# Conv + two MLPs on one core: the taps' softmax laid on all channels, warm-up products put first, x turned in transpose mode, block 0's taps shared between VectorE and TensorE

## The chip, the cores and the metric

The kernel runs on 1 core of a Trainium2 chip. The metric is the device time in microseconds, lower is better. PE is TensorE (PEld its weight loads), DVE is VectorE, ACT is ScalarE, POOL is GpSimd, SP is the engine that issues most DMAs (SPq and ACTq are the queues of SP and ACT).

## The reference

```python
# x (2, 4096, 192) f32; weight (8 heads, 7 taps); head h owns channels 24h to 24h+23
w = softmax(weight, axis=-1)                   # exp(w - max) / (sum + 1e-9)
out[s, c] = sum_k w[head(c), k] * x_pad[s + k, c]   # causal, 6 zeros in front
x = out.reshape(8192, 192)
h = x @ w_in;  x = maximum(0.01 * h, h) @ w_out       # 192 -> 2048 -> 192
h = x @ w_in2; g = where(h >= 1, h, where(h <= -1, 0, (h + 1)**2 / 4))
return g @ w_out2
```

## The kernel before, in words

The tokens are cut into 16 blocks of 512 (`T`). In a block the channels lie on the partitions: part 0 holds channels 0 to 127, part 1 the other 64, twice. A block's convolution (`add_conv`) loads x, turns it so that channels lie on partitions (tile `xT`), and adds up seven taps (`tap`: ACT does tap 0, DVE the others, one dependent instruction each at L505). `add_split` then writes the sum as a high half (ACT, L409) and a low half (DVE or POOL, L413) in a reduced format (fp32r), for three to five cheap products instead of one dear one.

A unit `(m, j, f)` is one slice of 128 hidden values of MLP m for block j. It has five "up" products (L549), an activation (ACT twice at L573 and DVE at L577 for the first MLP; the tiles are `gh` and `gl`), and five "down" products (L558). There are 512 units, so 5120 such products of 128x512. A unit's up products need their share of the split input weights (`wi_h`, `wi_l`, `wi_b`), its down products that of the output weights (`wo_h`, `wo_l`, `wo_b`). `add_weights` splits both, in groups that serve two values of f: ACT L248, DVE L261, L252 and L255, POOL L265, ACT L276, then subtractions on POOL or DVE (L281).

The first three blocks (`early`, j < N0 = 3) run side by side through the first MLP; `OFF = (0, 1, 4)` says by how many f each starts behind block 0. Here x is loaded in natural layout by SP (L451) and turned by eight products with the identity (L461); part 1 takes its seven taps from four fp32 products on PE (`tap_pair`, L511) with diagonal matrices that ACT fills (L390). In this stretch the up products have two banks of PSUM (`h_bank`), and there are four buffers each of `gh` and `gl`; so only some four units can be up ahead of their down products. After 48 units (`FULL`) the two MLPs alternate.

`add_taps` makes the softmax on 8 partitions (one head each) and spreads it to the channels by two products with a 0/1 matrix `heads` (L349). `add_warm` gives PE 17 products of zeros (L311), which the planner may put where PE has nothing else.

Every step is handed to a planner (`Plan`) with an engine, a cost and what it needs. It goes backwards from due times (a unit's up products are due at 2330 ns times its number) to each step's latest start, `late`, and then makes a list schedule: an engine that is free takes, of the steps that are ready by then, the one with the earliest `late`. This order is what each engine executes, in order; the costs and latencies (`HOP`, `SAME`, `DMA_LATENCY`) shape it but are not waited for on the chip.

Of the kernel before, what the change touches and what calls it, by code (L numbers as in the profile page):

```python
# [17 lines left out]
HOP, SAME, DMA_LATENCY = 220, 130, 2600  # L18
# [15 lines left out]
class Plan:  # L34
# [42 lines left out]
    def order(self):  # L77
        steps = self.steps
        after = [[] for _ in steps]
        left = []  # L80
        for s in steps:
            s["deps"].discard(s["n"])
            left.append(len(s["deps"]))
            for d in s["deps"]:
                after[d].append(s["n"])

        topo, count = [s["n"] for s in steps if not s["deps"]], list(left)
        for n in topo:
# [49 lines left out]
        self.start = start  # L138
        return sorted(done, key=lambda n: start[n])
# [3 lines left out]
def kernel(  # L143
# [26 lines left out]
    PAD = K - 1  # L170
    NS = T // 128
# [8 lines left out]
    OFF = (0, 1, 4)  # L180
    N0 = len(OFF)

# [4 lines left out]
    WARM = 17  # L187
# [31 lines left out]
    def add_weights(t, m, o, g):  # L219
# [47 lines left out]
        plan.add(dma, 450 if o else 1500, load, writes=[raw])  # L267
        plan.add(act, 550, lower, reads=[raw], writes=[ba])
        plan.add(dve, 360, rest, reads=[raw], writes=[bp])
        plan.add(dve, 360, shift, reads=[ba], writes=[bf])  # L270
        plan.add(dve, 560, sign, reads=[raw, bf], writes=[bf])
# [13 lines left out]
        if o == 0:  # L285
# [6 lines left out]
            for e in range(2):  # L292
                r = slice(DB * e, DB * (e + 1))
                q = slice(DB * (1 - e), DB * (2 - e))
                sub(dve, 300, wi_b[m][q, 2 * g + e], lambda r=r: ba()[r, 256:CW], wi_b[m][r, 2 * g + e], 1)
# [8 lines left out]
    def add_warm():  # L304
        zero = cp.tile([128, 128], mybir.dt.bfloat16, name="zero")
        nc.vector.memset(zero, 0.0)
        out_ = bank(7, -10)
        for _ in range(WARM):
            plan.add(
                pe, 430,  # L310
# [4 lines left out]
                writes=[out_], due=1e9,  # L315
# [3 lines left out]
    def add_taps():  # L319
        raw = cp.tile([H, K], F32, name="raw_taps")  # L320
        top = cp.tile([H, 1], F32, name="top")
        tot = cp.tile([H, 1], F32, name="tot")
        heads = cp.tile([H, 256], F32, name="heads")
        spread = bank(5, -9)

        def mark():

            own = heads[:, 0:D]
            nc.gpsimd.memset(own, 1.0)
            for base, sign in ((0, 1), (G - 1, -1)):  # L330
                nc.gpsimd.affine_select(
                    out=own, in_=own, compare_op=ALU.is_ge, fill=0.0, base=base, pattern=[[sign, D]],
                    channel_multiplier=-sign * G,
                )
            nc.gpsimd.tensor_copy(heads[:, D:], heads[:, 128:D])

        def shift():
            nc.vector.tensor_reduce(out=top, in_=raw, axis=AX.X, op=ALU.max)
            nc.vector.tensor_scalar(raw, raw, top, None, ALU.subtract)

        def norm():
            nc.vector.tensor_reduce(out=tot, in_=raw, axis=AX.X, op=ALU.add)
            nc.vector.tensor_scalar(tot, tot, 1e-9, None, ALU.add)
            nc.vector.reciprocal(out=tot, in_=tot)
            nc.vector.tensor_scalar(raw, raw, tot, None, ALU.mult)

        def to_channels():
            for i in range(2):
                nc.tensor.matmul(  # L349
                    out=spread()[:, K * i:K * (i + 1)], lhsT=heads[:, 128 * i:128 * (i + 1)], rhs=raw,  # L350
                    start=True, stop=True,
                )

        k = "raw_taps"

        nc.sync.dma_start(out=raw, in_=weight)
        nc.vector.memset(half, 0.5)
        nc.scalar.activation(out=tot, in_=half[0:H], func=ACTF.Exp)
        plan.add("taps", 100, lambda: None, writes=[k])
        plan.steps[-1]["lag"] = DMA_LATENCY  # L360
        plan.add(pool, 900, mark, writes=["heads"])
        plan.add(dve, 250, shift, reads=[k], writes=[k])
        plan.add(act, 150, lambda: nc.scalar.activation(out=raw, in_=raw, func=ACTF.Exp), reads=[k], writes=[k])
        plan.add(dve, 500, norm, reads=[k], writes=[k])
        plan.add(pe, 300, to_channels, reads=[k, "heads"], writes=[spread], due=-1e6)
        plan.add(
            dve, 80,
            lambda: nc.vector.tensor_copy(taps.rearrange("p i k -> p (i k)"), spread()[:, 0:2 * K]),
            reads=[spread], writes=["taps"],
        )  # L370

        def pairs():

            nc.vector.tensor_copy(pair[0:DB], spread()[0:DB, K:2 * K:2])
            nc.vector.tensor_copy(pair[DB:, 0:NP - 1], spread()[DB:, K + 1:2 * K:2])

        nc.vector.memset(pair, 0.0)
        plan.add(dve, 160, pairs, reads=[spread], writes=["pair"])

    def add_diagonals():  # L380
# [5 lines left out]
        plan.add(pool, 260, fold, reads=["ident"], writes=["same"])  # L386
        for k in range(NP):
            plan.add(
                act, 400,
                lambda k=k: nc.scalar.activation(  # L390
                    out=flat(k).rearrange("p (e d) -> p e d", e=2), in_=same.unsqueeze(1).broadcast_to((128, 2, DB)),
                    func=ACTF.Copy, scale=pair[:, k:k + 1],
# [9 lines left out]
    def flat(k):  # L402
        return spare()[:, 0, 128 * k:128 * (k + 1)].bitcast(F32)
# [13 lines left out]
    def add_conv(at, j):  # L417


        early = j < N0  # L420
# [5 lines left out]
        def halo():  # L426
# [6 lines left out]
            old, before = xT[j - 1](), int(j - 1 < N0)  # L433
            if before == back == 0:
                nc.gpsimd.tensor_copy(t()[:, :, 0:PAD], old[:, :, T:T + PAD])
                return
            nc.gpsimd.tensor_copy(t()[:, 0, 0:PAD], old[:, 0, T:T + PAD])
            nc.gpsimd.tensor_copy(t()[low, 1, 0:PAD], old[low, 1, T:T + PAD])
            c = T + back - before
            nc.gpsimd.tensor_copy(t()[high, 1, 0:PAD - back], old[high, 1, c:c + PAD - back])  # L440
# [3 lines left out]
            pool, 1700 if early else 240, halo, reads=old, writes=[(t, 0), (t, 1)], uses=[t] + [k[0] for k in old[:1]]  # L444
        )
        if early:
# [3 lines left out]
                dma, 700,  # L450
# [3 lines left out]
            plan.steps[-1]["lag"] = DMA_LATENCY + 1100  # L454
            turned = [bank(i, at) for i in CONV_BANKS[j]]

            for i, (c, n_c) in enumerate(((0, 128), (128, DB))):
                for n in range(NS):
                    plan.add(
                        pe, 215,  # L460
                        lambda i=i, n=n, c=c, n_c=n_c: nc.tensor.matmul(  # L461
                            out=turned[i]()[0:n_c, 128 * n:128 * (n + 1)], lhsT=v()[:, n, c:c + n_c], rhs=ident,
                            start=True, stop=True,
# [50 lines left out]

        for i in range(2):
# [7 lines left out]
            else:  # L523
                plan.add(act, 710, lambda i=i: tap(i, 0), reads=[(t, i), "taps"], writes=[y], uses=[t])
                for k in range(1, K):
                    plan.add(
                        dve, 740, lambda i=i, k=k: tap(i, k), reads=[(t, i), y], writes=[y], uses=[t],
                        chain=(y, "taps"),
                    )
# [5 lines left out]
    def add_unit(t, u):  # L535
# [27 lines left out]
        for part in range(2):  # L563
            plan.add(
                pe, (2 if part else 3) * PASS, lambda part=part: up(part), reads=[(src, 2 * part), (src, 2 * part + 1), (key, part)],
                writes=[h, (h, part)], uses=[src], due=UNIT * t, chain=(h, "up"),
# [152 lines left out]
```

## Time and profile before

| | us |
|---|---|
| median of 3 runs | 1236.08 (1236.07 to 1236.96) |
| the profiled execution | 1235.87 |
| its span | 1234.2 |
| PE busy in it | 1221.1 (99%) |
| DVE busy | 792.6 (64%) |
| ACT busy | 737.5 (60%) |
| POOL busy | 426.7 (35%) |

The span is the part of the execution that the engines' records cover; 1.7 us lie around it. All positions in rows are microseconds from the start of the span. A matmul's end is modelled, so a product of 128x512 shows 0.39 us while the next starts 0.23 us behind it.

### The profile page before, as it was taken

The numbers are of one execution on the slowest core, as the hardware profiler recorded it, in microseconds if no ns is written. First come the engines' busy times: TensorE is split into PE (matmuls) and PEld (weight loads), VectorE is DVE, ScalarE is ACT, GpSimd is POOL, SyncE is SP. The second block draws the span as 40 slices with busy tenths as digits, with TensorE's granted clock in tenths as the row PEclk, the third lists the DMA queues.
The fourth block names the chain that finished last, engine by engine and source line by source line (L and its number), as shares of the span: only waits on it lengthen the run. The fifth ranks groups of instructions, "written<-read, shape, count | busy, mean of one in ns | idle before, by whom it ended". The sixth has DMA issues, their size and how long they took to land.

```text
span 1234.2 us, 15412 instructions
## 1 busy us (share of the span) xinstructions
PE 1221.1 (99%) x5213; PEld 972.2 (79%) x5213; DVE 792.6 (64%) x1234; ACT 737.5 (60%) x1293; POOL 426.7 (35%) x379
## 2 busy tenths in 40 slices
PE   8999999999999999999999999999999999999997
PEld 5777887888888888888888888888888888888886
DVE  7998895847557484664847558485574544446664
ACT  6677866656556565655656555565555656556554
POOL 5555463323223232232322323223232222225554
PEclk9999999999999999999999999999999999999999
DMA  5333300101001010010101001010000000000000
GB/s 146 94 96 102 82 1 9 31 1 22 9 9 22 1 22 10 9 22 1 27 4 18 13 6 25 1 22 1 1 13 1 14 1 5 10 1 14 13 14 14
DMA packets 116496, 27.88 MB, mean 23 GB/s; under 512 B 106688, under 2 KB 114368, under 8 KB 116416
## 3 DMA queue, kind: packets, MB, share of 16 engines
q1 hardware_dynamic: 115360, 26.76, 10.5%
q8 instruction: 41, 0.67, 0.2%
q14 instruction: 39, 0.32, 0.1%
q10 hardware_dynamic: 1056, 0.13, 0.1%
HBM read 20.58 MB, written 6.29 MB: 22 GB/s over the span
## 4 chain that ended last, share of the span: by engine, by line
PE 92%; DVE 5%; issue 1%; DMA 0%; ACT 0%; SPq 0%; POOL 0%; DVEq 0%; POOLq 0%
PE bank L558 46%; PE bank L549 46%; DVE xy L505 2%; DVE gl L577 1%; DVE wp L261 1%; DVE wf L255 0%; DVE wf L252 0%; DMA wraw<-in_moe_w_out_dram 0%; DVE wi_b L281 0%; DVE x L413 0%; DVE xT L495 0%; POOL wa L265 0%; SPq L240 0%; ACT xT L474 0%; SPq L451 0%
## 5 line engine op out<-in xcount | busy, mean ns | idle before, releaser
L597 POOL TENSOR_TENSOR gl<-g,gh 128x512 fp32r<-128x512 f32 x256 | 340.1, 1330 | 694.2 <-ACT gh L595 683.4
L584 DVE TENSOR_SCALAR s<-bank 128x512 f32<-128x512 f32 x256 | 176.2, 689 | 338.6 <-PE bank L549 337.8
L549 PE MATMUL bank<-x,wi_h 128*128 128x512 f32 x1024 | 323.7, 397 | 3.6 <-DVE gl L577 3.6
L549 PE MATMUL bank<-x,wi_b 128*128 128x512 f32 x1024 | 321.6, 395 | 0.0
L588 ACT ACTIVATE s<-s,half 128x512 f32<-128x512 f32 x256 | 185.2, 724 | 204.5 <-DVE s L584 201.3
L595 ACT CAST gh<-g 128x512 fp32r<-128x512 f32 x256 | 158.7, 620 | 167.9 <-DVE g L592 161.4
L549 PEld LDWEIGHTS bank<-x,wi_h 128*128 128x128 f32 x1024 | 191.4, 188 | 54.3 <-DVE gl L577 8.2
L549 PEld LDWEIGHTS bank<-x,wi_b 128*128 128x128 f32 x1024 | 192.2, 188 | 46.7
L592 DVE TENSOR_TENSOR g<-bank,s 128x512 f32<-128x512 f32 x256 | 175.0, 684 | 65.9 <-ACT s L588 65.9
L558 PE MATMUL bank<-gl,wo_b 128*128 128x512 f32 x512 | 202.6, 396 | 1.7 <-DVE gl L577 1.7
L558 PE MATMUL bank<-gh,wo_h 128*128 128x512 f32 x512 | 202.6, 396 | 0.0
L549 PE MATMUL bank<-x,wi_l 128*128 128x512 f32 x512 | 202.3, 395 | 0.0
L558 PE MATMUL bank<-gh,wo_l 128*128 128x512 f32 x512 | 202.2, 395 | 0.0
L558 PE MATMUL bank<-gh,wo_b 128*128 128x512 f32 x512 | 202.2, 395 | 0.0
L558 PE MATMUL bank<-gl,wo_h 128*128 128x512 f32 x512 | 202.2, 395 | 0.0
L573 ACT ACTIVATE gh<-bank 128x512 fp32r<-128x512 f32 x256 | 152.8, 597 | 74.3 <-PE bank L558 37.2
L577 DVE TENSOR_TENSOR gl<-bank,gh 128x512 fp32r<-128x512 f32 x256 | 173.9, 679 | 6.3 <-ACT bank L573 6.1
L573 ACT ACTIVATE bank<-bank 128x512 f32<-128x512 f32 x256 | 151.1, 590 | 0.3
L505 DVE SCALAR_TENSOR_TENSOR xy<-xT,taps,xy 128x512 f32<-128x512 f32 x174 | 145.9, 866 | 0.3
L558 PEld LDWEIGHTS bank<-gl,wo_b 128*128 128x128 f32 x512 | 96.1, 188 | 26.3 <-DVE gl L577 3.0
L558 PEld LDWEIGHTS bank<-gh,wo_l 128*128 128x128 f32 x512 | 96.1, 188 | 23.6 <-issue 0.2
L558 PEld LDWEIGHTS bank<-gh,wo_h 128*128 128x128 f32 x512 | 96.1, 188 | 23.6 <-issue 0.2
(76 smaller groups left out, 728.0 us busy)
## 6 DMA issues: line engine op xcount, KB each, us to landing
xy<-in_x_dram SPq DMA_DIRECT2D x104, 64.0 KB, 2.4
wraw<-in_moe_w_out_dram SPq DMA_DIRECT2D x16, 384.0 KB, 3.1
out_dram<-o SPq DMA_DIRECT2D x94, 64.0 KB, 2.0
wraw<-in_moe_w_in_dram SPq DMA_DIRECT2D x16, 256.0 KB, 3.1
wraw<-in_moe_w_in_dram SPq DMA_DIRECT2D x32, 64.0 KB, 2.7
wraw<-in_x_dram SPq DMA_DIRECT2D x3, 384.0 KB, 3.5
out_dram<-o ACTq DMA_DIRECT2D x2, 64.0 KB, 2.5
raw_taps<-in_weight_dram SPq DMA_DIRECT2D x1, 0.2 KB
```

What stands on the lines that cost most here:

```text
L261: nc.vector.tensor_scalar(bp(), raw()[:, :, 0], 2.0 ** -29, None, ALU.mult)
L505: nc.vector.scalar_tensor_tensor(out=ys[i](), in0=t()[:, i, k:k + T], scalar=taps[:, i, k:k + 1], in1=ys[i](), op0=ALU.mult, op1=ALU.add,)
L549: nc.tensor.matmul(out=h(), lhsT=w, rhs=v[:, k], start=(part == 0 and i == 0), stop=(part == 1 and i == 1))
L558: nc.tensor.matmul(out=p[part](), lhsT=w, rhs=v(), start=(first and i == 0), stop=(last and i == len(todo) - 1))
L573: lambda dst=dst: nc.scalar.activation(out=dst(), in_=h(), func=ACTF.Prelu, alpha=0.01),
L577: dve, 680, lambda: nc.vector.tensor_tensor(out=b(), in0=h(), in1=a(), op=ALU.subtract),
L584: dve, 680, lambda: nc.vector.tensor_scalar(s(), h(), 1.0, -1.0, ALU.min, ALU.max),
L588: act, 720, lambda: nc.scalar.activation(out=s(), in_=s(), func=ACTF.Square, scale=0.5, bias=half),
L592: dve, 680, lambda: nc.vector.tensor_tensor(out=g(), in0=h(), in1=s(), op=ALU.max),
L595: plan.add(act, 620, lambda: nc.scalar.copy(a(), g()), reads=[g], writes=[a])
L597: pool, 1390, lambda: nc.gpsimd.tensor_tensor(out=b(), in0=g(), in1=a(), op=ALU.subtract),
```

## The change

- The softmax: the taps are loaded to all 128 partitions by a broadcast DMA on ACT's queue (before: 8 partitions, SP's queue, first in it), DVE multiplies them with a mask `own` of the head of each channel and adds up, and the softmax runs on 128 x 2 x 7. The products that spread it are gone.
- Warm-up: 24 products instead of 17; 11 of them stand first on PE, 13 are fillers. POOL clears their operand; their bank is 1 (that of unit 1) instead of 7.
- The turning products become `nc.tensor.transpose`.
- Block 0, part 0: taps 4 to 6 become three fp32 products on PE with diagonals of their own (`tap_a`), and one DVE addition brings them in; DVE keeps taps 1 to 3.
- The seven diagonals are filled by DVE (before: four, by ACT).
- The halo copies of early blocks 1 and 2 go from POOL to ACT.
- `OFF` becomes `(0, 2, 4)`.
- The planner gets other costs and a look ahead: a step that is ready within `SOON` = 200 ns may be taken before one that is ready now.

```diff
-HOP, SAME, DMA_LATENCY = 220, 130, 2600
+HOP, SAME, DMA_LATENCY = 220, 130, 2200
+SOON = 200
...
-            n = min((n for n in q if ready[n] <= at), key=lambda n: (late[n], n))
+            n = min((n for n in q if ready[n] <= at + SOON), key=lambda n: (late[n], n))
+            at = max(at, ready[n])
...
+    KP = 4
-    OFF = (0, 1, 4)
+    OFF = (0, 2, 4)
+    E0 = 3
-    WARM = 17
+    COLD, WARM = 11, 24
...
-        nc.vector.memset(zero, 0.0)
-        out_ = bank(7, -10)
+        nc.gpsimd.memset(zero, 0.0)
+        out_ = bank(1, -10)
...
-                writes=[out_], due=1e9,
+                writes=[out_], due=-1e9 if cold else 1e9,
...
+            for rows, i in ((slice(0, 128), 0), (slice(0, DB), 1)):
+                for base, sign in ((128 * i, 1), (G - 1 - 128 * i, -1)):
+                    nc.gpsimd.affine_select(out=own[rows, i], ...)
+            nc.gpsimd.tensor_copy(own[DB:, 1], own[0:DB, 1])
+        def choose():
+            nc.vector.tensor_tensor(out=wide, in0=raw..., in1=own..., op=ALU.mult)
+            nc.vector.tensor_reduce(out=taps, in_=wide, axis=AX.X, op=ALU.add)
+            nc.vector.tensor_reduce(out=top, in_=taps, axis=AX.X, op=ALU.max)
+            nc.vector.tensor_tensor(out=taps, in0=taps, in1=top..., op=ALU.subtract)
...
-        nc.sync.dma_start(out=raw, in_=weight)
+        nc.scalar.dma_start(out=raw, in_=weight.rearrange("h k -> (h k)").partition_broadcast(128))
...
-        plan.add(pe, 300, to_channels, reads=[k, "heads"], writes=[spread], due=-1e6)
+        plan.add(dve, 600, choose, reads=["raw_taps", "own"], writes=["taps"], due=-2e6)
...
+        for k in range(KP, K):
+            plan.add(dve, 220, lambda k=k: nc.vector.tensor_scalar(flat(NP + k - KP), ident, taps[:, 0, k:k + 1], None, ALU.mult), ...)
         for k in range(NP):
-                act, 400,
-                lambda k=k: nc.scalar.activation(...)
+                dve, 220,
+                lambda k=k: nc.vector.tensor_scalar(...)
...
-            pool, 1700 if early else 240, halo, ...
+            act if early and j else pool, 600 if early else 240, halo, ...
...
-                        pe, 215,
-                        lambda ...: nc.tensor.matmul(out=turned[i]()[...], lhsT=v()[...], rhs=ident, ...)
+                        pe, 60,
+                        lambda ...: nc.tensor.transpose(turned[i]()[...], v()[...], ident)
...
+        def tap_a(k):
+            nc.tensor.matmul(out=rest(), lhsT=flat(NP + k - KP), rhs=t()[:, 0, k:k + T], start=(k == KP), stop=(k == K - 1))
...
+                    for k in range(KP, K):
+                        plan.add(pe, 870, lambda k=k: tap_a(k), ...)
-                for k in range(1, K):
+                for k in range(1, KP if shared else K):
...
+                        dve, 690, lambda: nc.vector.tensor_tensor(out=y0(), in0=rest(), in1=y0(), op=ALU.add),
```

## Rows read from the trace of the kernel before

**Rows 1.** The page, part 1: busy us, share of the span, instructions.
```profile
PE 1221.1 (99%) x5213; PEld 972.2 (79%) x5213; DVE 792.6 (64%) x1234; ACT 737.5 (60%) x1293; POOL 426.7 (35%) x379
```
**Rows 2.** Windows: stretch, us, busy of PE, PEld, DVE, ACT, POOL, clock, DMA, GB/s.
```profile
19.00:30.00 11.00, 8.20 (x38) 5.69 (x39) 10.91 (x20) 8.72 (x20) 6.02 (x10) 1.00 0.37 110
30.00:60.00 30.00, 29.25 (x117) 21.31 (x116) 29.68 (x52) 21.30 (x47) 17.05 (x18) 1.00 0.36 97
60.00:130.00 70.00, 68.03 (x289) 53.42 (x288) 64.57 (x113) 51.18 (x116) 36.87 (x42) 1.00 0.34 98
130.00:1228.00 1098.00, 1097.72 (x4704) 882.51 (x4702) 673.20 (x1021) 644.65 (x1089) 357.81 (x285) 1.00 0.07 12
```
**Rows 3.** Chain that ended last, its last 14 us: start, us, what.
```profile
1222.07 5.85 PE bank L558 x25
```
**Rows 4.** PE's waits over the whole span: total us, times, longest.
```profile
PE bank L549 <- DVE gl L577: 3.6, 7, 0.9
PE bank L558 <- DVE gl L577: 1.7, 3, 0.7
```
**Rows 5.** PE's timeline, 16 to 62 us: start, us, instruction, idle before it.
```profile
15.80 2.74 PE L511 MATMUL bank<-xT,x 128*128 128x512 f32 x6
...
18.83 0.79 PE L549 MATMUL bank<-x,wi_h 128*128 128x512 f32 x2
...
24.58 0.73 PE L549 MATMUL bank<-x,wi_h 128*128 128x512 f32 x2 [0.82 <-DVE gl L577]
...
29.92 0.40 PE L558 MATMUL bank<-gh,wo_b 128*128 128x512 f32 x1
...
38.65 0.40 PE L558 MATMUL bank<-gh,wo_b 128*128 128x512 f32 x1
```
**Rows 6.** POOL's timeline, 14 to 45 us.
```profile
17.33 1.73 POOL L413 TENSOR_TENSOR x<-xy,x 128x512 fp32r<-128x512 f32 x1
...
28.73 0.73 POOL L281 TENSOR_TENSOR wo_l<-wa,wo_h 128x256 fp32r<-128x256 f32 x1
...
37.47 0.73 POOL L281 TENSOR_TENSOR wo_l<-wa,wo_h 128x256 fp32r<-128x256 f32 x1
```
**Rows 7.** DVE's timeline, 14 to 45 us.
```profile
23.25 0.70 DVE L495 STREAM_TRANSPOSE xT<-xy 128x512 f32<-128x512 f32 x1
...
24.45 1.11 DVE L255 SCALAR_TENSOR_TENSOR wf<-wraw,wf 128x384 uint32<-128x384 uint32 x1
```
**Rows 8.** All engines' timeline, 0 to 16 us.
```profile
0.82 0.40 SPq L356 DMA_DIRECT2D raw_taps<-in_weight_dram  x1
...
1.07 3.88 PE L311 MATMUL bank<-zero 128*128 128x512 bf16 x10 [1.07 <-DVE pair L377]
...
2.18 0.15 DVE L338 TENSOR_REDUCE top<-raw_taps 8x1 f32<-8x7 f32 x1 [1.15 <-DMA raw_taps<-in_weight_dram]
...
5.41 3.26 PE L461 MATMUL bank<-ident,wraw 128*128 128x128 f32 x24
...
6.61 0.59 ACT L468 COPY xT<-bank 128x512 f32<-128x512 f32 x1 [0.18 <-PE bank L461]
7.40 0.56 ACT L248 ACTIVATE wa<-wraw 128x384 f32<-128x384 f32 x1 [0.20 <-DMA wraw<-in_moe_w_in_dram]
7.42 0.36 DVE L261 TENSOR_SCALAR wp<-wraw 128x384 uint32<-128x384 uint32 x1 [1.50 <-DMA wraw<-in_moe_w_in_dram]
...
7.86 0.71 ACT L501 ACTIVATE xy<-xT,taps 128x512 f32<-128x512 f32 x1
...
9.55 4.86 DVE L505 SCALAR_TENSOR_TENSOR xy<-xT,taps,xy 128x512 f32<-128x512 f32 x5
...
11.10 0.65 POOL L437 COPY xT<-xT 128x6 f32<-128x6 f32 x1
```
**Rows 9.** Tile wraw, 0 to 45 us: PE's loads of it, ns min/median/max.
```profile
L461 PEld LDWEIGHTS bank<-ident,wraw x48: 132/162/192, 5.4 to 23.4; 128*128 128x128 f32 x24, 128*64 128x64 f32 x24
```
**Rows 10.** Line L505, 0 to 31 us: ns min/median/max.
```profile
L505 DVE SCALAR_TENSOR_TENSOR xy<-xT,taps,xy x15: 736/750/1371, 9.6 to 30.4; 128x512 f32<-128x512 f32 x15
```

More of the change, by code (lines that the diff above doesn't have):

```diff
@@ L305, in add_warm @@
         zero = cp.tile([128, 128], mybir.dt.bfloat16, name="zero")
-        nc.vector.memset(zero, 0.0)
-        out_ = bank(7, -10)
-        for _ in range(WARM):
+        nc.gpsimd.memset(zero, 0.0)
+        out_ = bank(1, -10)
+        for i in range(WARM):
+            cold = i < COLD
             plan.add(
-                pe, 430,
+                pe, 430 if cold else 220,
                 lambda: nc.tensor.matmul(
@@ L326, in mark @@
+        wide = cp.tile([128, 2, K, H], F32, name="wide")
+        top = cp.tile([128, 2], F32, name="top")
         def mark():
-            own = heads[:, 0:D]
             nc.gpsimd.memset(own, 1.0)
[L330 to L335, printed above, removed]
@@ L354, in add_taps @@
-        k = "raw_taps"
-        nc.sync.dma_start(out=raw, in_=weight)
-        nc.vector.memset(half, 0.5)
[L358 to L363, printed above, removed]
@@ L364, in add_taps @@
-        plan.add(dve, 500, norm, reads=[k], writes=[k])
-        plan.add(pe, 300, to_channels, reads=[k, "heads"], writes=[spread], due=-1e6)
+            for rows, i in ((slice(0, 128), 0), (slice(0, DB), 1)):
+                for base, sign in ((128 * i, 1), (G - 1 - 128 * i, -1)):
+                    nc.gpsimd.affine_select(
+                        out=own[rows, i], in_=own[rows, i], compare_op=ALU.is_ge, fill=0.0, base=base,
+                        pattern=[[-sign * G, H]], channel_multiplier=sign,
+                    )
@@ new lines, in mark @@
+            nc.gpsimd.tensor_copy(own[DB:, 1], own[0:DB, 1])
+        def choose():
+            nc.vector.tensor_tensor(
+                out=wide, in0=raw.rearrange("p (h k) -> p k h", k=K).unsqueeze(1).broadcast_to((128, 2, K, H)),
+                in1=own.unsqueeze(2).broadcast_to((128, 2, K, H)), op=ALU.mult,
+            )
+            nc.vector.tensor_reduce(out=taps, in_=wide, axis=AX.X, op=ALU.add)
+            nc.vector.tensor_reduce(out=top, in_=taps, axis=AX.X, op=ALU.max)
+            nc.vector.tensor_tensor(
+                out=taps, in0=taps, in1=top.unsqueeze(2).broadcast_to((128, 2, K)), op=ALU.subtract
+            )
@@ new lines, in norm @@
+        def norm():
+            nc.vector.tensor_reduce(out=top, in_=taps, axis=AX.X, op=ALU.add)
+            nc.vector.tensor_scalar(top, top, 1e-9, None, ALU.add)
+            nc.vector.reciprocal(out=top, in_=top)
+            nc.vector.tensor_tensor(out=taps, in0=taps, in1=top.unsqueeze(2).broadcast_to((128, 2, K)), op=ALU.mult)
+        nc.scalar.dma_start(out=raw, in_=weight.rearrange("h k -> (h k)").partition_broadcast(128))
+        nc.vector.memset(half, 0.5)
+        nc.scalar.activation(out=top[:, 0:1], in_=half, func=ACTF.Exp)
@@ L366, in add_taps @@
+        nc.vector.memset(pair, 0.0)
+        plan.add("taps", 100, lambda: None, writes=["raw_taps"])
+        plan.steps[-1]["lag"] = 1500
+        plan.add(pool, 1300, mark, writes=["own"])
+        plan.add(dve, 600, choose, reads=["raw_taps", "own"], writes=["taps"], due=-2e6)
         plan.add(
-            dve, 80,
-            lambda: nc.vector.tensor_copy(taps.rearrange("p i k -> p (i k)"), spread()[:, 0:2 * K]),
-            reads=[spread], writes=["taps"],
+            act, 200, lambda: nc.scalar.activation(out=taps, in_=taps, func=ACTF.Exp), reads=["taps"], writes=["taps"]
@@ L370, in add_taps @@
         )
+        plan.add(dve, 500, norm, reads=["taps"], writes=["taps"])
         def pairs():
[L374 to L378, printed above, removed]
+            nc.vector.tensor_copy(pair[0:DB], taps[0:DB, 1, 0:K:2])
+            nc.vector.tensor_copy(pair[DB:, 0:NP - 1], taps[DB:, 1, 1:K:2])
@@ L380, in add_diagonals @@
+        plan.add(dve, 250, pairs, reads=["taps"], writes=["pair"])
     def add_diagonals():
@@ L386, in add_diagonals @@
         plan.add(pool, 260, fold, reads=["ident"], writes=["same"])
+        for k in range(KP, K):
+            plan.add(
+                dve, 220,
+                lambda k=k: nc.vector.tensor_scalar(flat(NP + k - KP), ident, taps[:, 0, k:k + 1], None, ALU.mult),
+                reads=["ident", "taps"], writes=[("diagonal a", k)], uses=[spare],
+            )
         for k in range(NP):
             plan.add(
-                act, 400,
-                lambda k=k: nc.scalar.activation(
-                    out=flat(k).rearrange("p (e d) -> p e d", e=2), in_=same.unsqueeze(1).broadcast_to((128, 2, DB)),
-                    func=ACTF.Copy, scale=pair[:, k:k + 1],
+                dve, 220,
+                lambda k=k: nc.vector.tensor_scalar(
+                    flat(k).rearrange("p (e d) -> p e d", e=2), same.unsqueeze(1).broadcast_to((128, 2, DB)),
+                    pair[:, k:k + 1], None, ALU.mult,
                 ),
@@ L417, in add_conv @@
     def add_conv(at, j):
-        early = j < N0
+        early = j < E0
         xT[j] = t = buf("xT", at, [128, 2, PAD + T])
@@ L432, in halo @@
                 return
-            old, before = xT[j - 1](), int(j - 1 < N0)
+            copy = nc.scalar.copy if early else nc.gpsimd.tensor_copy
+            old, before = xT[j - 1](), int(j - 1 < E0)
             if before == back == 0:
-                nc.gpsimd.tensor_copy(t()[:, :, 0:PAD], old[:, :, T:T + PAD])
+                copy(t()[:, :, 0:PAD], old[:, :, T:T + PAD])
                 return
-            nc.gpsimd.tensor_copy(t()[:, 0, 0:PAD], old[:, 0, T:T + PAD])
-            nc.gpsimd.tensor_copy(t()[low, 1, 0:PAD], old[low, 1, T:T + PAD])
+            copy(t()[:, 0, 0:PAD], old[:, 0, T:T + PAD])
+            copy(t()[low, 1, 0:PAD], old[low, 1, T:T + PAD])
             c = T + back - before
-            nc.gpsimd.tensor_copy(t()[high, 1, 0:PAD - back], old[high, 1, c:c + PAD - back])
+            copy(t()[high, 1, 0:PAD - back], old[high, 1, c:c + PAD - back])
         old = [] if j % PER == 0 else [(xT[j - 1], 0), (xT[j - 1], 1)]
         plan.add(
-            pool, 1700 if early else 240, halo, reads=old, writes=[(t, 0), (t, 1)], uses=[t] + [k[0] for k in old[:1]]
+            act if early and j else pool, 600 if early else 240, halo, reads=old, writes=[(t, 0), (t, 1)],
+            uses=[t] + [k[0] for k in old[:1]],
         )
@@ L524, in add_conv @@
                 plan.add(act, 710, lambda i=i: tap(i, 0), reads=[(t, i), "taps"], writes=[y], uses=[t])
-                for k in range(1, K):
+                shared = j == 0 and i == 0
+                if shared:
+                    rest = bank(CONV_BANKS[0][0], at + 1)
+                    for k in range(KP, K):
+                        plan.add(
+                            pe, 870, lambda k=k: tap_a(k), reads=[("diagonal a", k), (t, 0)], writes=[rest],
+                            uses=[t, spare], chain=(rest, "taps"),
+                        )
+                for k in range(1, KP if shared else K):
                     plan.add(
-                        dve, 740, lambda i=i, k=k: tap(i, k), reads=[(t, i), y], writes=[y], uses=[t],
+                        dve, 780, lambda i=i, k=k: tap(i, k), reads=[(t, i), y], writes=[y], uses=[t],
                         chain=(y, "taps"),
+                    )
+                if shared:
+                    plan.add(
+                        dve, 690, lambda: nc.vector.tensor_tensor(out=y0(), in0=rest(), in1=y0(), op=ALU.add),
+                        reads=[y, rest], writes=[y], chain=(y, "taps"),
                     )
@@ L565, in add_unit @@
                 pe, (2 if part else 3) * PASS, lambda part=part: up(part), reads=[(src, 2 * part), (src, 2 * part + 1), (key, part)],
-                writes=[h, (h, part)], uses=[src], due=UNIT * t, chain=(h, "up"),
+                writes=[h, (h, part)], uses=[src], due=UNIT * t - (HEAD if t == 0 else 0), chain=(h, "up"),
             )
```

42 lines of the change are left out of this document (13 added, 29 removed).

## The prediction

> **What bounds the kernel now.** I read the page first: PE is busy for 99% of the span [rows 1]. The windows then say how even that is: from 130 us to 1228 us PE is idle for 0.28 us in 1098, and 4704 products in that time make 0.2334 us a product [rows 2]. So 5120 products want 5120 x 0.2334 = 1195 us, whatever else is changed, and the last of them ends at 1222.07 + 5.85 = 1227.9 [rows 3]. The change leaves the products of the units and what follows the last one as they are; everything it can give lies ahead of 130 us.
>
> There the reader is to see three things. First, PE's first unit starts at 18.83 [rows 5], and its second product, the one that reads the low half, waits for POOL's subtraction, which ends at 17.33 + 1.73 = 19.06 [rows 6]. A gapless stream from 19.0 would be done at 19.0 + 1195 = 1214; the true end is 13.9 us later. Second, of this 13.9 us some 3.4 are block 2's four fp32 pair products (the six records of such products that start at 15.80 last 2.74 in all, 0.43 a record, two records a product [rows 5], so 8 x 0.43) and 2.2 its eight turning products (24 records, two a product, in 3.26 us [rows 8]: 0.27 each). The other 8.3 is PE waiting: the list of waits has 5.3 us, all for DVE's `gl` [rows 4], and since a product's modelled end lies 0.16 us behind the next one's usual start, some ten such waits hide another 1.6. Third, DVE is the engine that is full: busy 10.91 of 11 us from 19 to 30 and 29.68 of 30 us from 30 to 60, while PE loses 2.80 and 0.75 there, and 1.97 from 60 to 130 [rows 2].
>
> The wait from 24.58 on looks like one for `gl` [rows 5], but what ends the state is another thing: the first down product stands at 29.92, and the weights it lacks, `wo_l`, are done at 28.73 + 0.73 = 29.46 [rows 5, 6]. Until then some five units' up products are all that PE may do. So the first true bound of the stretch is the chain to the first `wo_l`: DVE's L255 for it runs from 24.45 to 25.56 [rows 7], then POOL, ACT and POOL again, 3.9 us. DVE gets to it late because it must first do the convolutions of blocks 0 and 1 and two other groups of weights.
>
> **The change, part by part.** *Start of PE.* Ten warm-up products run from 1.07 to 4.95 [rows 8], then the spreading products and at 5.41 the first turn. Eleven products without the spreading end about 5.1 (one more at 0.22 to 0.43, less the hidden 0.16), so turning starts some 0.3 earlier. The 13 fillers must be done before unit 1, as they share its bank: 13 x 0.22 = 2.9 us of PE, against 1.5 of the seven before. PE is free enough between 5 and 14: turning, 7 fp32 products at 0.86 and the fillers are about 11 us of work, part of which fits behind unit 0. I take nothing for it; without that cover it is up to 1.4 us.
>
> *Turning.* No row shows a transpose; it is bounded by 0.27 (as now [rows 8]) and zero. Each still loads 128 columns of weights, 0.13 to 0.19 us [rows 9], now once instead of twice; I take 0.14. Four turns are then 0.56 in place of 1.08, and ACT's copy to `xT` starts at about 5.75 instead of 6.61 [rows 8]. [...]
>
> *Tap 0.* ACT's copy takes 0.59, so tap 0 could run from 6.4 to 7.1; before, the lowering of the first weights (7.40, 0.56) slipped in ahead of it and it stood at 7.86 [rows 8]. It needs the taps. The softmax: the load goes from SP's queue to ACT's, at about the same 0.82, and landed 1.36 us later before [rows 8]; for 128 partitions I bound it by 1.4 and 3.5. POOL's mask is six instructions on a few elements; the nearest row is a small POOL copy at 0.65 [rows 8], so from 0.9 on it is done by 4.8 at the latest; I take 3. Then four DVE steps, Exp, four DVE steps; the nearest DVE row is 0.15 [rows 8], so with hops about 2 us: taps at 5 to 6.5. Hidden behind turn and copy, with nothing to spare at the upper end. SP's first x load leaves 0.45 earlier [rows 8]. ACT's queue: the load's issue (0.40) delays its table load and a dummy Exp, which nothing waits for before 3 us.
>
> *Diagonals.* Seven on DVE; bounds: 0.15 (smallest row) and 0.36 (a scaling of 128x384 [rows 8]); I take 0.2, 1.4 us. DVE has nothing from the softmax to 7.42, when the first weights land [rows 8]; if the taps come at 6.5 instead, up to 1.4 us of it lands on DVE's full stretch. ACT is rid of four, and takes six small halo copies from POOL, which cost POOL up to 0.65 each at 11.10 [rows 8]: about even for ACT.
>
> *Block 0's taps.* DVE's first five taps took 4.86 us, 0.97 each [rows 8], while POOL was busy; its median there is 0.75 [rows 10]. Three leave DVE: 2.3 to 2.9 us, less the addition, priced as a subtraction of that shape at 0.7: 1.6 to 2.2, I take 1.9. The three products on PE (3 x 0.86) run beside DVE's three taps.
>
> *DVE's stream.* Before, DVE had done 1.6 us of weight work between 7.42 and its first tap at 9.55; as a full stream it would have begun at 7.9. Now it begins at 7.1: 0.8 earlier. With 1.9 less work, and about 0.5 for POOL being out of the taps' way (between nothing and 0.7), the L255 of the first output weights ends 3.2 us sooner, and the first down product with it: 29.9 becomes 26.7. I bound this by 1.0 (late taps, diagonals in the full stretch) and 5.0. Unit 0 itself starts near 14.5, but that alone brings nothing: what PE does early it spends waiting later.
>
> *OFF.* With (0, 2, 4) block 1 starts at unit 3 instead of 2, block 2 at unit 8 instead of 9, and the second and third groups of weights are due one unit (2.33 us) sooner. The second `wo_l` was done at 38.20, the product that follows at 38.65 [rows 5, 6]: no slack there. This costs 0 to 2.3; block 1's six taps being due later gives DVE the same amount to spend on weights, so I take nothing.
>
> *Planner.* SOON lets an engine wait up to 0.2 us for an urgent step rather than start a long idle one, such as the transpose of a later block at 23.25, 0.70 us, while `gl` was due [rows 7]. The waits from 30 to 130 are 2.72 us [rows 2] and the hidden part. I take 1.2 back, bounded by -1 (PE itself made to wait) and 3.
>
> *Sum.* 3.2 + 1.2 = 4.4: the profiled execution's 1235.87 becomes 1231.5; the median lies 0.2 above it, so 1231.7. The upper limit: PE has no use for more than the 8.3 of waiting and the 2 of shorter turns, so not under 1226.
>
> **Rivals.** *Weights bind (no change).* DVE's relief is real but the output weights still come as late, because the second group is due a unit sooner and the diagonals fall into the full stretch: 3.2 - 1.4 - 2.3 and nothing from the planner, 1236.4. For it: `wo_l` ended within 0.5 us of its use twice. Against it: DVE's work before that point does shrink.
>
> *All the waits go.* The stream starts at 14.5 and the planner's order holds: 3.2 to 5.0 and 3.0 of the later waits: 1227.9. Against it: DVE stays full from 7 to 60.
>
> *Slower.* The list schedule, with its new due times, does the third input group and block 2's taps (both due a unit sooner) before the first output group on DVE and POOL. Its place is the first `wo_l`; each microsecond that it ends past 29.46 costs one, less the 1.2 from later. At 32 it is slower by more than the measurement can tell; one group's DVE and POOL chain in front (3.9 us) on today's time makes 1235.9 + 3.9 - 1.2 = 1238.6, a little more with both.
>
> [...]
>
> **How the numbers follow.** Chances: forecast 0.55 (its own range 1229.5 to 1233.5), no change 0.20 (1233.5 to 1237.5), all the waits 0.12 (1226.5 to 1229.5), clock 0.05, slower 0.08. About 0.2%, 2.5 us, is what a measurement tells from no change: faster is under 1233.6, slower above 1238.6. Faster: 0.54 + 0.12 + 0.03 = 0.69; slower: 0.07; same: the rest, 0.24. The range runs from 1228.0, leaving out half of the best case, to 1236.0, leaving out the slower case and part of no change.
>
> **What would show it.** Right: the first turn near 5.1 with records of 0.07 to 0.2; tap 0 before 7.5; diagonals done by then; unit 0 before 15.5; the first L558 at 25 to 28; the same 0.2334 a product after 130; less than 2.7 of waits from 30 on. Wrong: the first L558 at 29 or later, products of 512 columns at 0.43 after the turns, PE's queue standing at a fp32 tap while unit 0 is ready, or new waits past 130 us.

## The result and the profile after

The changed kernel takes 1200.31 us (median; 1200.16 to 1201.27) against 1236.2 for the kernel before beside it: the ratio is 0.971 [0.9697, 0.9722], 35.9 us less. The forecast was 4.4 us less. The profiled execution took 1200.22 with a span of 1198.5.

The page of the kernel after, part 1, answers to [rows 1]:

```profile
PE 1187.3 (99%) x5198; PEld 971.7 (81%) x5198; DVE 798.0 (67%) x1239; ACT 734.4 (61%) x1295; POOL 423.3 (35%) x376
```

PE is as full as before and has almost the same number of instructions, but is busy for 34 us less. The windows of the kernel after say where (columns as in [rows 2]):

```profile
60.00:130.00 70.00, 69.28 (x303) 56.40 (x303) 67.90 (x118) 54.41 (x120) 33.47 (x38) 1.00 0.34 98
130.00:1190.00 1060.00, 1059.46 (x4675) 877.57 (x4674) 674.70 (x1021) 638.30 (x1085) 360.74 (x288) 1.00 0.07 12
400.00:800.00 400.00, 400.00 (x1766) 331.48 (x1765) 254.89 (x384) 239.26 (x406) 120.01 (x93) 1.00 0.08 13
```

The second row is the surprise. 4675 products in 1060 us are 0.2267 each, where [rows 2] have 0.2334, at the same granted clock of 1.00 and with 0.54 us idle. The same stretch of the kernel before holds 50 products fewer, also with PE never idle:

```profile
400.00:800.00 400.00, 400.00 (x1716) 321.81 (x1715) 243.44 (x368) 230.54 (x388) 115.15 (x91) 1.00 0.08 12
```

The mean from start to start of successive products between 400 and 1000 us is 233.33 ns before and 226.67 ns after. Every kind of product, up or down, has the new value. 4704 products behind 130 us times 6.67 ns are 31.4 us, and 31.4 + 4.4 = 35.8. The question is why products that the diff does not touch run faster.

Nothing in the diff's text touches these products, but the built program has their operands elsewhere. The softmax's small tiles stand in front of the working tiles in each partition's memory, and the new set is 352 bytes smaller. Byte addresses in a partition, with the remainder by 256 (of the two built programs; the profile holds no addresses, but the 352 bytes and the remainders against the weights follow from the sizes of the kernels' tiles):

```
tile            before             after
wi_h, wo_h ..   16512 + 8192 k  128   the same       128
gh (first)      179680          224   179328         128
gl (first)      187872          224   187520         128
x1 (first)      196064          224   195712         128
x2 (first)      145888          224   137344         128
```

The tiles that PE streams (`x`, `gh`, `gl`) moved against the weights that it loads. Below, **distance** is the streamed tile's address less that of the weights, modulo 256 bytes: 96 before, 0 after.

### The profile page after: what moved, and what is told of

Its sections match the earlier page's. It is cut to its first block, busy times and chain, and to the rows that moved or that the text cites. A ratio compares the mean times of both kernels' runs of the same rounds, so it can differ in the third digit from the quotient of the medians.

```text
span 1198.5 us, 15406 instructions
## 1 busy us (share of the span) xinstructions
PE 1187.3 (99%) x5198; PEld 971.7 (81%) x5198; DVE 798.0 (67%) x1239; ACT 734.4 (61%) x1295; POOL 423.3 (35%) x376
## 4 chain that ended last, share of the span: by engine, by line
PE 89%; DVE 4%; POOL 1%; issue 1%; ACT 1%; SPq 0%; DMA 0%; DVEq 0%; ACTq 0%; POOLq 0%
PE bank L585 44%; PE bank L576 44%; DVE xy L515 1%; DVE gl L604 1%; DVE wp L270 1%; DVE s L611 0%; DVE g L619 0%; POOL gl L624 0%; POOL wa L274 0%; DVE wi_b L290 0%; SPq L496 0%; DVE wf L264 0%; DVE wf L261 0%; DMA xy<-in_x_dram 0%; DVE x L423 0%
## 5 line engine op out<-in xcount | busy, mean ns | idle before, releaser
L576 PE MATMUL bank<-x,wi_h 128*128 128x512 f32 x1024 | 317.2, 391 | 2.3 <-DVE gl L604 2.2
L576 PE MATMUL bank<-x,wi_b 128*128 128x512 f32 x1024 | 316.3, 390 | 0.2 <-DVE x L423 0.2
L585 PE MATMUL bank<-gl,wo_b 128*128 128x512 f32 x512 | 199.5, 390 | 0.5 <-POOL gl L624 0.5
L585 PE MATMUL bank<-gh,wo_b 128*128 128x512 f32 x512 | 199.5, 390 | 0.0
L585 PE MATMUL bank<-gl,wo_h 128*128 128x512 f32 x512 | 199.5, 390 | 0.0
L576 PE MATMUL bank<-x,wi_l 128*128 128x512 f32 x512 | 199.5, 390 | 0.0
L585 PE MATMUL bank<-gh,wo_l 128*128 128x512 f32 x512 | 199.4, 389 | 0.0
```

What stands on the lines that cost most here:

```text
L576: nc.tensor.matmul(out=h(), lhsT=w, rhs=v[:, k], start=(part == 0 and i == 0), stop=(part == 1 and i == 1))
L585: nc.tensor.matmul(out=p[part](), lhsT=w, rhs=v(), start=(first and i == 0), stop=(last and i == len(todo) - 1))
```

## The experiments

A pad is a dead tile of N bytes a partition in the pool of constants. In front of `xT, x1, x2 = {}, {}, {}` it moves the streamed tiles and leaves the weights; in front of `wi_h = [...]` it moves both. The other working tiles move with the streamed ones.

**1. Is it the addresses?** First theory: the streamed tiles must lie on a multiple of 64 bytes. Three kernels:

```diff
+    cp.tile([128, 8], F32, name="pad")     # e1: before + 32; e2: after + 32; e4: after, [128, 16], + 64
```

> The kernel before with 32 unused bytes in front of the working tiles, nothing else: the columns that stream through PE (x, gh, gl) then start at a multiple of 64 bytes in each partition, as in the changed kernel, instead of 32 bytes behind one. Address theory: products start 226.7 ns apart instead of 233.3 everywhere after 130 us, 5120 x 6.67 ns = 34 us less, 1202 us; order of work and first unit unchanged. Transpose-mode theory (turning by ordinary fp32 products leaves PE in a slower state): 1236, 233.3 ns. Order theory (the new order of the instructions streams better): 1236, 233.3 ns.

> The changed kernel with 32 unused bytes in front of the working tiles, so that they stand where they stood modulo 64 before the change. Address theory: 233.3 ns a product, 1200 + 34 = 1234 us; what is left to the stated edits themselves is then under 3 us. Transpose-mode and order theories: 1200 us, 226.7 ns.

> The changed kernel with 64 unused bytes in front of the working tiles: still multiples of 64, but no longer of 128. Address theory with pieces of 64 bytes: 226.7 ns, 1200 us. Address theory with pieces of 128 bytes or more: slower than 226.7 ns, by 16 columns' time (6.7 ns, 1234 us) or more. Theory that any shift of the tiles matters through other engines' traffic: some third time.

Measured: e1 1231.83 us, ratio 0.9959 [0.9944, 0.9974], 232.38 ns a product; e2 1232.73, 0.9966 [0.9953, 0.9979], 233.33 ns; e4 1211.52, 0.9795 [0.9781, 0.981], 228.89 ns. Thirty-two dead bytes take 32 us off the changed kernel's gain, without touching an instruction: the rate hangs on where the tiles lie. But 64-alignment is not the rule: e1 is aligned and slow, e4 is aligned and neither.

**2. Is it the transpose mode?** The turn as the ordinary product again:

```diff
-                        nc.tensor.transpose(turned[i]()[0:n_c, 128 * n:128 * (n + 1)], v()[:, n, c:c + n_c], ident)
+                        nc.tensor.matmul(out=turned[i]()[...], lhsT=v()[:, n, c:c + n_c], rhs=ident, start=True, stop=True)
```

> The changed kernel with x turned by ordinary products again; its tiles stand where the changed kernel's do. Transpose-mode theory: 233.3 ns a product and 1234 us. Address theory and order theory: 226.7 ns, 1200 to 1203 us (24 turns at 0.27 instead of about 0.16 us, 1.3 at most of it on the way to unit 0).

Measured: 1201.7, 0.9714 [0.9698, 0.973], 226.67 ns. The mode has no part in the rate. What it is worth besides is too little to tell: 1.4 us by the medians, 0.5 by the ratios, and the intervals overlap.

**3. Does the kernel before get the rate by its place alone?** 160 bytes bring its streamed tiles to distance 0:

```diff
+    cp.tile([128, 40], F32, name="pad")     # before + 160
```

> The kernel before with 160 unused bytes in front of the working tiles: the streamed tiles x, gh and gl then start at 128 modulo 512 bytes, exactly where the split weights start modulo 512 and where the changed kernel has them. Distance theory (PE reads the next weights while it streams, and the two reads collide by the distance of their addresses modulo 512): 226.7 ns a product and 1202 us, the whole gain but for the stated edits. Theory that the old order of instructions is what streams badly: 233 ns, 1232 to 1236.

Measured: 1205.18 against 1236.84 for the kernel before beside it, 0.9745 [0.9731, 0.976], 226.67 ns. The windows of this kernel, from 400 to 800 us:

```profile
400.00:800.00 400.00, 400.00 (x1766) 331.32 (x1765) 251.89 (x382) 237.35 (x401) 118.63 (x93) 1.00 0.08 13
```

The kernel before, with its order, softmax and turns as they were, has the 1766 products of the kernel after. The move alone is worth 31.7 us.

**4. The streamed tiles' own place, or that against the weights?**

```diff
+    cp.tile([128, 16], F32, name="pad_w")   # f2: after, weights and all behind them + 64; f4: [128, 8], + 32
+    cp.tile([128, 112], F32, name="pad")    # f3: this as well; streamed + 512 in all, weights + 64
```

> The changed kernel with weights and streamed tiles both moved by 64 bytes: distance 0 kept, the place itself changed as in the earlier run with 64 bytes. Distance theory: 226.7 ns, 1200 us. Absolute theory (where the streamed tile starts modulo 128 or more): 228.9 ns, 1211.5 us as in that run.

> The changed kernel with the weights alone moved by 64 bytes; the streamed tiles move by 512, the same place modulo 512. Distance theory: another rate than 226.7 ns, likely that of a distance of 64, 228.9 ns and 1211 us. Absolute theory: 226.7 ns, 1200 us.

> The changed kernel with weights and streamed tiles both moved by 32 bytes: distance 0, both 32 bytes behind a multiple of 64. Pure distance theory: 226.7 ns, 1200 us. A theory of distance plus alignment to 64: 233.3 ns, 1233 us.

Measured: f2 1200.97, 0.9716 [0.9702, 0.9731], 226.67 ns; f4 1202.23, 0.9721 [0.9707, 0.9736], 226.67 ns; f3 1231.96, 0.9963 [0.9948, 0.9977], 233.33 ns. The windows of f3, from 400 to 800 us:

```profile
400.00:800.00 400.00, 400.00 (x1716) 320.54 (x1716) 243.66 (x367) 231.07 (x388) 117.35 (x91) 1.00 0.07 12
```

Both moved together: the full rate, also 32 bytes off any 64-alignment. The weights moved by 64 against the stream: 1716 products, as before. It is the distance that counts, and its sign too: f3 was expected at the 228.89 ns of e4, but the weights moved by 64 make a distance of 192, not of 64.

**5. How does the rate run over the distance?**

```diff
+    cp.tile([128, 40], F32, name="pad")     # k1: after + 160; k2: [128, 56], + 224; g2: [128, 64], + 256
```

> The changed kernel with streamed tiles 256 bytes further, weights in place: distance 256 modulo 512. If the collisions repeat every 256 bytes: 226.7 ns, 1200 us. If every 512 or more: another rate, between 216 ns (no collision at all, 1146 us) and 233.3 ns (1233 us); the rows so far give 228.9 at 64, 233.3 at 32, 352 and 448, 232.4 at 384.

> The changed kernel, streamed tiles 160 bytes further: distance 160 modulo 256. The rates so far: 226.7 ns at 0 and 256, 228.9 at 64, 232.4 at 128, 233.3 at 32, 96 and 192. By the odd multiples of 32 so far: 233.3 ns, 1233 us. If the collisions are only with the stream's place some columns behind: a rate of its own, down to 216 ns (1146 us).

> The same at distance 224. By the odd multiples of 32: 233.3 ns, 1233 us; the same way out as for 160.

Measured: g2 1200.33, 0.9705 [0.9692, 0.9719]; k1 1237.06, 1.0006 [0.9997, 1.0016]; k2 1232.51, 0.997 [0.9958, 0.9981]. All the moves together:

```
distance   ns a product   us        kernel
0          226.67         1200.3    after, g2 (+ 256); f2 1201.0, f4 1202.2, f1 1205.2
32         233.33         1232.7    e2
64         228.89         1211.5    e4
96         233.33         1236.2    before
128        232.38         1231.8    e1 (before + 32)
160        234.29         1237.1    k1
192        233.33         1232.0    f3
224        233.33         1232.5    k2
```

The rows of 96 and 128 and f1 have the order of the kernel before, which costs 4 to 5 us more; the rates compare all the same. With 160 bytes of dead memory the whole change measures as no change. Distance 0 is the best of the eight, 64 is two thirds as good, and the other six lie together.

**6. Does each product follow its own two operands?** A gap of 64 bytes before `gh` and of 192 before `x1` moves `gh` and `gl` by 64 and leaves `x1` at distance 0:

```diff
+    gaps = dict(gh=16, x1=48)
...
+            if tag in gaps:
+                sp.tile([128, gaps.pop(tag)], F32, tag="gap_" + tag, bufs=1, name="gap_" + tag)
```

> The changed kernel with gh and gl alone 64 bytes further; x and the weights stay at distance 0. Theory that the collision is between one product's stream and the load of the next product's weights: up products (x) stay near 226.7 ns, down products (gh, gl) go to about 228.9, 227.8 on average, 1205.9 us. Theory that one common state of PE sets the rate: one rate for both, 226.7 or 228.9 (1200 or 1211.5 us).

Measured: 1218.95, 0.9859 [0.9844, 0.9874], a mean of 230.67 ns. From the start of a product of `gh` or `gl` to the next start it took 231.7 to 236.7 ns, with one kind at 225.8 (`gl` with `wo_h`); from one of `x` with `wi_h` and `wi_l` 230.8, with `wi_b` 226.7. Neither theory holds: products whose own operands did not move got slower, and mixed distances are worse than 64 throughout.

**7. What the edits of the start are worth.** Four kernels, one line each; e7 leaves the load of the taps out and fills the tile with 0.25, so that all taps weigh alike:

```diff
+        nc.gpsimd.memset(raw, 0.25)         # e7, in place of the broadcast load
+    OFF = (0, 1, 4)                         # e8
+SOON = 0                                    # e9
+        nc.sync.dma_start(out=raw, ...)     # m1: the broadcast load on SP's queue, ahead of x
```

> The changed kernel with the taps' broadcast load left out; POOL fills the raw taps with a constant, so the convolution weighs all taps alike. In the changed kernel the load landed 3.8 us after its issue, x's first load 5.2 us after its own (3.3 before the change), and DVE's softmax started at 4.75. Theory that the broadcast load holds up x and the taps: x lands by 4.6 to 5.0, diagonals are done before 7.5 instead of 10.0, the first down product comes 1 to 2.5 us sooner and the time falls by as much. Rival (the time is set by DVE's work behind it): first turns sooner, but under 0.5 us of time.

> The changed kernel with OFF = (0, 1, 4) as before; tiles at the same places. The prediction took nothing for OFF, bounded by a cost of 2.3 us and as much gain. If block 1's taps being due later is what helps: 1 to 2.5 us slower than the changed kernel. If the weights being due a unit sooner costs: 0.5 to 2.3 us faster.

> The changed kernel with SOON = 0: an engine takes only steps that are ready, as before, with the new costs. The prediction gave the planner 1.2 us (from -1 to 3). If the look ahead is what took PE's waits between 30 and 130 us from 3.6 us to 0.9: those waits are back and the time is 1.2 to 3 us longer. If it is the new costs or block 0's shorter chain: within 0.5 us.

> The changed kernel with the taps' broadcast load on SP's queue ahead of everything, alone in flight for some 0.45 us. With the load behind x, x landed 1.8 us sooner and the time did not move (1200.1); with no load at all it fell by 2.1. So it should be the taps' landing, 4.6 us into the span, that costs. Theory: being first, the taps land by 2.5 to 3.5 and most of the 2.1 us comes back, 1198.3 to 1199.5. Rival: the broadcast needs its 3.8 us wherever it stands, and x leaves 0.45 later: 1200 to 1201 us.

Measured: e7 1198.22, 0.9689 [0.9675, 0.9702]; e8 1201.2, 0.9713 [0.97, 0.9726]; e9 1204.19, 0.9736 [0.9723, 0.9749]; m1 1200.3, 0.9709 [0.9695, 0.9723]. So against the changed kernel's 1200.3 the broadcast load costs 2.1 us, `OFF` gains 0.9, which is within the spread of the runs, and the look ahead 3.9. And the load put behind x's first load on SP's queue:

```diff
+                lambda: (nc.sync.dma_start(out=v(), in_=x[...]), [f() for f in late_loads if j == 0]),
```

> The changed kernel with the taps' broadcast load on SP's queue, right behind x's first load, instead of on ACT's queue beside it; plan and tiles unchanged. Leaving the load out gave 2.1 us and let x land 3.1 us after its issue instead of 5.2. Theory that the small descriptors on a second queue, ahead of x, hold it up: x lands at about 3.3, the taps no later than now (4.6), and 1 to 2 us are gained, 1198.5 to 1199.5 us. Theory that the broadcast itself is slow wherever it stands: the first weights, queued behind it, and the taps land later, 1200 to 1202 us.

Measured: 1200.14, 0.9707 [0.9693, 0.9722]: no difference. From issue to landing, in the lists of DMA issues of the kernel after, h1, m1 and e7 in this order:

```profile
wraw<-in_x_dram SPq DMA_DIRECT2D x1, 384.0 KB, 5.2
raw_taps<-in_weight_dram ACTq DMA_DIRECT2D x1, 28.0 KB, 3.8
```
```profile
wraw<-in_x_dram SPq DMA_DIRECT2D x1, 384.0 KB, 3.4
raw_taps<-in_weight_dram SPq DMA_DIRECT2D x1, 28.0 KB, 3.4
```
```profile
raw_taps<-in_weight_dram SPq DMA_DIRECT2D x1, 28.0 KB, 3.9
```
```profile
wraw<-in_x_dram SPq DMA_DIRECT2D x1, 384.0 KB, 3.1
```

The broadcast load needs 3.9 us even when it is the first thing in the queue, and 3.4 behind x (1.36 before, for eight rows). On a queue of its own it also goes with a load of x that lands 5.2 us after issue, against 3.1 without it. So it is the taps' lateness that costs: in h1 x landed 1.8 us sooner and nothing was gained, but DVE's softmax still began at 4.78 (4.75 in the kernel after), while in e7 its last step was done at 4.54 (6.95 in the kernel after).

## Why the prediction was wrong, and where it was right

**The step that failed** is the first one: "The change leaves the products of the units and what follows the last one as they are; everything it can give lies ahead of 130 us." The instructions were left as they are; their operands were not. 0.2334 us a product was taken as a constant of the product [rows 2], without a reason, and the limit of 1226 and all the rivals were built on it. It belongs to a distance of 96. At distance 0 it is 0.2267: f1 shows it without any edit of the change (31.7 of the 35.9 us), and f2, f3 and e2 from the other side. That the pool of constants changes its size stood in the diff (the mask `own`, the product tile, the spreading matrix gone); I read it for its instructions alone.

**The sum of the edits was right in size.** At equal rates it can be measured twice: e2 against the kernel before is 4.2 us faster (both at 233.33 ns), the kernel after against f1 4.9, or 4.3 by their ratios (both at 226.67 ns). The forecast was 4.4. All this holds to about half a microsecond, as the kernel before came out at 1236.1 to 1237.1 beside the different runs.

**Its terms were not**, though, so that the agreement is luck. The timeline of all engines of the kernel after, from 0 to 20 us:

```profile
1.07 4.87 PE L321 MATMUL bank<-zero 128*128 128x512 bf16 x11 [1.07 <-POOL own L337]
...
4.75 0.35 DVE L347 TENSOR_TENSOR wide<-raw_taps,own 128x112 f32<-128x112 f32 x1 [3.77 <-DMA raw_taps<-in_weight_dram]
...
6.11 1.41 PE L472 MATMUL bank<-ident,wraw 128*128 128x128 f32 x8 [0.16 <-DMA wraw<-in_x_dram]
...
7.20 0.55 ACT L257 ACTIVATE wa<-wraw 128x384 f32<-128x384 f32 x1 [1.06 <-DMA wraw<-in_moe_w_in_dram]
...
7.78 0.59 ACT L478 COPY xT<-bank 128x512 f32<-128x512 f32 x1
...
8.45 0.72 ACT L511 ACTIVATE xy<-xT,taps 128x512 f32<-128x512 f32 x1
...
9.74 0.28 DVE L400 TENSOR_SCALAR x<-same,pair 128x128 f32<-128x128 f32 x1
9.94 3.39 DVE L515 SCALAR_TENSOR_TENSOR xy<-xT,taps,xy 128x512 f32<-128x512 f32 x3
...
16.64 0.82 PE L576 MATMUL bank<-x,wi_h 128*128 128x512 f32 x2
```

- *Start of PE.* First turn at 6.11, forecast 5.1. The eleven warm-up products took 4.87, all of them slow (0.40 to 0.43 from start to start; of the ten before, the last three lay 0.22 to 0.32 apart), and x landed only at 0.82 + 5.2 = 6.0.
- *Turning.* Four turns took 0.81 (the first starts at 6.11, the fifth at 6.92), not 0.56: the first starts lie 0.21 to 0.24 apart and only those behind 0.11, where I took 0.14. Before, a turn was two records of 0.11. The 0.07 that the prediction names as the least for a record is shown by no run; the trace has 0.11, half of before.
- *Tap 0.* 8.45, not 6.4 to 7.5. The load landed 3.8 us after its issue, beyond the 3.5 by which I had bounded it, and the softmax could start only at 4.75. But that is not what held tap 0: the taps were done at 6.95. It followed ACT's copy of the turned x at 7.78, and that stood in ACT's order behind the lowering of the first weights, for which ACT had waited 1.06 us. An earlier tap 0 would not have helped either: in h1 it stands at 7.75 and the time is the same. The late softmax held DVE, which goes from it to the diagonals and the weights almost without a pause.
- *Diagonals.* 0.28 each, not 0.2, and done at 10.0: they fell, as the unfavourable bound had it, into DVE's full stretch. Its first tap starts at 9.94, later than the 9.55 of before [rows 8]; I had put the stream 0.8 earlier.
- *Block 0's taps.* Three in 3.39, 1.13 each, where 0.75 to 0.97 had been the price: the relief was there, but the three that stayed took longer. The addition took 0.69, as priced. Unit 0 is at 16.64, 2.2 us ahead of before [rows 5], but not in 14.5 to 15.5.
- *First output weights.* POOL's timeline of the kernel after, from 13 to 28 us, and PE's from 16 to 48:

```profile
26.85 0.45 POOL L290 TENSOR_TENSOR wo_b<-wa,wo_b 128x128 fp32r<-128x128 f32 x1
```
```profile
27.68 0.74 PE L576 MATMUL bank<-x,wi_h 128*128 128x512 f32 x2 [1.32 <-DVE gl L604]
...
29.31 0.48 PE L585 MATMUL bank<-gh,wo_b 128*128 128x512 f32 x1
```

The weights are done at 27.30, 2.2 us ahead of 29.46 [rows 6]. But the first down product stands at 29.31, 0.6 ahead of before, not at the 26.7 of the 3.2 us; a first L558 at 29 or later was the prediction's own sign of being wrong. Ahead of it, in PE's order, an up product waits 1.32 for `gl`. The reading of the kernel before was wrong here too. Its PE timeline from 16 to 62 us:

```profile
29.11 0.74 PE L549 MATMUL bank<-x,wi_h 128*128 128x512 f32 x2 [0.85 <-DVE gl L577]
```

PE stood idle for `gl` ahead of this up product, and not again ahead of the down product at 29.92 [rows 5], whose own weights `wo_b` POOL had finished at 28.77. So `wo_l` at 29.46 was not the wait that ended last; `gl` was, before and after, and the term is 0.6 at this product. With the load left out (e7) weights (25.53) and product (27.53) both come 1.8 earlier.

- *Planner.* Taken at 1.2 with a bound of 3; e9 says 3.9. The windows of e9 for 60 to 130 us, and its first row of PE's waits:

```profile
60.00:130.00 70.00, 65.77 (x281) 51.53 (x281) 65.90 (x114) 50.80 (x114) 34.13 (x41) 1.00 0.34 98
```
```profile
PE bank L585 <- DVE gl L604: 4.6, 7, 1.2
```

PE loses 4.23 us there without the look ahead and 0.72 with it (69.28 of 70), against 1.97 before [rows 2] and 2.65 in f1, at the same rate as e9. The new order and costs would have been worse than the old in this stretch; `SOON` is what makes them better. PE's waits for DVE's `gl` at down products are gone from the list of the kernel after, which is headed by

```profile
PE bank L576 <- DVE gl L604: 2.2, 4, 1.3
```

- *OFF.* Taken at nothing within 0 to 2.3 of loss; it gains 0.9 (e8; its interval and that of the kernel after overlap).

In sum 3.2 + 1.2 was made of two errors that cancel: without the look ahead the edits give 1.0 us (e9 against f1), and the look ahead gives 3.9. And of the 8.3 us that the prediction called waiting, its rows cover 6.9 (5.3 + 1.6); 1.4 had no row.

**The rivals.** *Weights bind* and *slower* did not come: e2, at the rate of before, is 4.2 us faster. *All the waits go* named 1227.9, which the rate alone undercuts; PE's idle 0.72 us from 60 to 130 and 0.54 from 130 to 1190 is near its picture, but the start is not. *The clock* (0.05 of the chances: PE, once up to speed, is slow again behind the turns) is shown by no run: the granted clock is 1.00 in every stretch up to 1190 us (also from 0 to 5 us, where products lie 0.40 to 0.43 apart, so that the spacing has to tell), the two warm-up products behind eight turns, at 7.35, lie 0.215 apart, and fp32 records 0.43, as before [rows 5]. The first turns, right behind the eleven slow warm-up products, are slow too (from the first to the fourth 0.21 to 0.24 apart), and the last four of the eight lie 0.11 apart. So the spacing halved among the turns themselves, and the seven later ones, behind 1.07 us of idle time, lie 0.11 to 0.17 apart.

**What is shown and what is not.** Shown is that the rate hangs on the distance (226.67 to 234.29 ns over the eight), is the same at 0 and 256 bytes (226.67), and that order, turns and softmax have no part in it. That the streamed tiles count, and not the others that a pad moves with them, is shown for `gh` and `gl` (k3), not for `x` by itself. The weights' last writes start at 189.8 us (POOL) and 188.0 us (ACT); of the groups by line of the kernel after the latest is

```profile
L290 POOL TENSOR_TENSOR wo_l<-wa,wo_h x16: 732/762/1189, 26.1 to 189.8; 128x256 fp32r<-128x256 f32 x16
```

So from 400 us on PE alone touches the weights. It loads the next weights while it streams the present tile (PEld is busy for 877.57 of the 1060 us, beside PE's 1059.46), and that the two get into each other's way is my guess from the distance. No run shows it: the streamed tiles are also written by ACT, DVE and POOL, and k3 fits no simple form of it. The starts say one thing more: at distance 96 intervals of 238, 230 and 232 ns follow each other in turn, at 64 of 226, 229 and 232, whatever kind of product it is. There a product's time goes by its place in the turn and not by its own operands, as if something were carried over from one product to the next. What it is that gives 0 and 256 bytes the same rate stays open.

## What to carry to other kernels

Where one engine streams for the whole span, work out its time for one instruction before and after any edit that adds or drops a tile: a changed rate with no idle time and the same clock came from the addresses here, not from the schedule. Try dead tiles of 32 to 224 bytes in front of the streamed tiles before (and after) judging an edit: on the kernel before one of 160 bytes is worth 31.7 us, seven times as much as all the edits here. And compare two versions at the same distance, or the placement's gain will be put down to the edit, or hide it.

## What the runs showed of the hardware that was not expected

- The product of 128x512 in fp32r takes 226.67, 228.89, 232.38, 233.33 or 234.29 ns from start to start, by the distance of its streamed tile from its weights modulo 256 bytes, with PE never idle and a granted clock of 1.00 from 400 to 800 us at seven of the eight distances tried (at 224 the runs show 1232.5 us and a mean clock of 0.999 to 1.00).
- At distance 96 the starts are not even: they lie 230 to 232 ns apart for two thirds of the products and 237 to 238 ns for the rest; at distance 0 all lie 225 to 228 ns apart.
- A broadcast load of 224 bytes to 128 partitions took 3.9 us to land first on SP's queue, 3.8 on ACT's and 3.4 behind x on SP's; the 384 KB load issued beside it on another queue took 5.2 us, against 3.1 without it.
- A turn of 128x128 in transpose mode took 0.11 us from start to start, and 0.21 to 0.24 right behind warm-up products that lay 0.43 apart; as an ordinary product, before, it was two records of 0.11 each.
